# Backward row layouts by DMA transposes, with a chunk's columns in blocked order

## The chip, the cores and the metric

The kernel runs on one core of a Trainium2 chip. The metric is the device time of one execution in microseconds (us); lower is better. A core has five instruction streams that matter here: TensorE (PE in the profile; its weight loads are PEld), VectorE (DVE), ScalarE (ACT), GpSimd (POOL) and SyncE (SP). SyncE does no arithmetic: in this kernel it issues most of the DMA transfers, all DMA transposes among them.

## The reference, cut to what matters

The reference is the forward pass of a small joint network and its gradient for all seven inputs. All tensors are bfloat16.

```python
h  = gelu(conv3(x,  w1))[:, ::2, :]        # B=2, T=16000, D=256, kernel of 3 taps
f  = gelu(conv3(h,  w2))[:, ::2, :]        # 4000 rows of f in each batch
fe = f @ w_f ;  ge = g @ w_g               # g: 8 rows in each batch
j  = tanh(fe[:, :, None, :] + ge[:, None, :, :])
out = j @ w_o                              # [2, 4000, 8, 256]
out, vjp = jax.vjp(forward, x, w1, w2, g, w_f, w_g, w_o)
return out, *vjp(grad_out)                 # grad_out: [2, 4000, 8, 256]
```

A matmul on TensorE contracts over the partition axis. The gradients of the activations contract over channels, so they need a tensor with channels on the partitions ("columns": one column for each time step). The gradients of the weights contract over time, so they need the same tensor with time steps on the partitions ("rows"). The whole argument is about how one is made from the other.

## The kernel before

The 4,000 time steps of each batch are worked off in chunks of up to 512. A small static scheduler (`op(engine, cost, ...)`) gives each operation its engine and its place in that engine's stream when the program is built. These are the parts that the change touches; `P` is 128, `KT` is 2 (256 channels are two halves of 128), `NB` is 4 blocks of 128 steps.

A row layout can be made in two ways. The first is a DMA transpose from SBUF to SBUF. If the buffer has exactly `n*P` columns, one transpose does both halves; a buffer with a padding column (for the neighbour that a 3-tap convolution needs) takes one transpose for each half:

```python
    def dma_rows(name, cls, g_, SRC, off, keys, nb=None, at=None):

        n = (chunks[g_][3] + off_extra.get(name, 0) * (chunks[g_][1] == last_ci[chunks[g_][0]]) + P - 1) // P
        R = buf(cls, [P, KT * NB * P], BF16, name)
        view = lambda: R[:, 0:KT * n * P].rearrange("p (k b q) -> p k b q", k=KT, q=P)
        R.rows = lambda m, bl: view()[:m, :, bl, :]
        R.cols = lambda m, bl, d2: view()[:m, d2, bl, :]
        st[g_][name] = R
        if SRC.shape[-1] == n * P:
            dma("SP", lambda: R[:].rearrange("p (g q) -> p g q", q=P), lambda: SRC[:].rearrange("p k w -> p (k w)"),
                r=[(SRC, k) for k in [0, 1] + keys], w=[R], bytes_=KT * n * P * P * 2, new=[R], transpose=True, nb=nb, at=at)
            return R
        for kt in range(KT):
            dma("SP", lambda kt=kt: view()[:, kt], lambda kt=kt: SRC[:, kt, off:off + n * P],
                r=[(SRC, k) for k in [kt] + keys], w=[(R, kt)], bytes_=n * P * P * 2, new=[R] if kt == 0 else [],
                transpose=True, nb=nb, at=at)
        return R
```

The second is TensorE: 128x128 transposes into PSUM, and a copy back into SBUF by ACT or DVE.

```python
    def to_rows(cls, SRC, off, n, keys):
        dst = buf(cls, [P, NB, D], BF16, cls.upper())
        dst.rows = lambda m, bl: dst[:m, bl, :]
        ps = psum(BF16)
        nbl = (n + P - 1) // P

        def trs(e):
            for bl in range(nbl):
                m = min(P, n - bl * P)
                for kt in range(KT):
                    nc.tensor.transpose(out=ps[:m, (bl * KT + kt) * P:(bl * KT + kt + 1) * P],
                                        in_=SRC[:, kt, off + bl * P:off + bl * P + m], identity=ident[:])
        op("PE", c_pe([P] * (nbl * KT)), trs, r=[(SRC, k) for k in keys] + [ident], w=[ps], new=[ps, dst])
        # [cut: evac() of ps into dst, on ACT or DVE]
```

Before, the row layouts of GHo and GHe (the gradients at the odd and even steps of h) take the second way:

```python
        GHoR = to_rows("rows", GHo, 0, Wsp, [0, 1, "z"])
        tick()
        GHeR = to_rows("rows", GHe, 1, Wsp, [0, 1, "z"])
        tick()
```

grad_out is read twice from DRAM: once as rows (GO_R) and once, transposed by the DMA on the way, as columns (GOT):

```python
    def load_got(g_, u, at):
        b, ci, c0, W = chunks[g_]
        GOT = buf("got", [P, KT, CW], BF16, "GOT")
        dma("SP", lambda: GOT[:, :, :W], lambda: grad_out[b, c0:c0 + W, u, :], r=[], w=[GOT], bytes_=W * D * 2, new=[GOT],
            transpose=True, at=at)
        st[g_].setdefault("GOT", {})[u] = GOT
```

A shifted tap reads the same padded buffer one column further on (`off` is 1 or 0):

```python
        gfk = [(GF, 0), (GF, 1), (GF, "h"), (GF, "z")]
        for mt in range(KT):
            ps = psum()

            def mms(e, mt=mt, ps=ps):
                for k, (i, off, kt) in enumerate([(i, off, kt) for i, off in ((0, 1), (2, 0)) for kt in range(KT)]):
                    mm(ps[:, :Ws], W2T[:, i, kt, mt * P:(mt + 1) * P], GF[:, kt, off:off + Ws], k == 0, k == 3)
            pe_first(mt == 0, "gho", c_pe([Ws] * 4), mms, r=gfk + [(WT, 1), (WT, 2)], w=[ps], new=[ps] + ([GHo] if mt == 0 else []))
            op("DVE", c_dve(Ws), lambda e, mt=mt, ps=ps: nc.vector.scalar_tensor_tensor(
                out=GHo[:, mt, 0:Ws], in0=S["G1o"][:, mt, 1:1 + Ws], scalar=1.0, in1=ps[:, :Ws], op0=ALU.add, op1=ALU.mult),
               r=[(S["G1o"], mt), (S["G1o"], "h"), ps], w=[(GHo, mt)])
            tick()
```

## Time and profile before

| | before |
|---|---|
| median of 4 runs | 820.42 us (820.27 to 822.75) |
| span in the profile | 817.6 us |
| busy: PE, DVE, ACT, POOL | 783.5, 749.1, 737.7, 184.1 us |
| sum of PE's work by columns | 774.6 us |
| DMA transposes and plain copies issued by SP | 351 and 215, issuing for 676 us |

The page's first part gives each engine's busy time, its share of the span and its instructions. The queue lines give packets, MB, and packet time as a share of the 16 DMA engines' time.

```profile
PE 783.5 (96%) x6082; PEld 580.1 (71%) x6172; DVE 749.1 (92%) x1703; ACT 737.7 (90%) x1198; POOL 184.1 (23%) x393
...
q1 hardware_dynamic: 347732, 128.93, 77.0%
```

Three engines stand at 90% or more, so the shares alone don't tell which binds. PE's list of waits does: in us in total, number of waits, longest. These are its first lines.

```profile
PE ps L308 <- DMA W<-in_w_dram: 3.0, 1, 3.0
PE GWO L308 <- ACT JR L628: 3.0, 4, 1.0
PE ps L308 <- DMA GOT<-in_grad_out_dram: 2.7, 1, 2.7
PE ps L308 <- DMA NFR<-NGFE: 1.8, 2, 1.6
PE ps L308 <- DMA GFR<-GF: 1.8, 2, 1.1
```

All lines of this list together are some 20 us of 818. Between 120 and 780 us PE is busy 653.76 of 660 us; the columns are window, length, then busy time and instructions of PE, PEld, DVE, ACT and POOL, PE's clock, DMA share and GB/s.

```profile
0.00:120.00 120.00, 101.72 (x707) 67.27 (x719) 100.68 (x248) 103.42 (x174) 25.65 (x56) 0.97 0.99 213
120.00:780.00 660.00, 653.76 (x5113) 489.72 (x5191) 625.21 (x1380) 619.58 (x995) 146.50 (x310) 1.00 1.01 227
```

A busy PE may still be a slow PE, so I also computed its least work. Starts of back-to-back matmuls stand 109 ns apart at 256 columns, 215 to 216 at 512 and 55 to 56 at 128, which is columns/2.4 + 2.5 ns. The Trainium skill ("TensorE: Matmul & The Clock Gate", section "Wait — 56ns, not 53.3ns?") states the same formula for a warm array, with a floor of about 25 ns; the trace agrees. Summed over the program's matmuls, this is 774.6 us. Time minus this work is time lost, and comparing the two at each weight load shows where: 28.0 us by the point where 120 us of work are done, only 3.2 us between 120 and 740 us of work, 4.0 us from there to the last matmul, and 7.7 us after it.

The groups that the change removes from PE and ACT, by shape (busy us, mean ns of one | idle before):

```profile
L502 PE MATMUL psb<-ident,GHo 128*128 128x128 bf16 x128 | 10.3, 219 | 0.0
L502 PE MATMUL psb<-ident,GHe 128*128 128x128 bf16 x128 | 10.1, 219 | 0.0
L316 ACT COPY ROWS<-psb 128x1024 bf16<-128x1024 bf16 x27 | 27.6, 1024 | 0.0
L316 ACT COPY ROWS<-psb 128x512 bf16<-128x512 bf16 x6 | 3.5, 584 | 0.6 <-PE psb L502 0.6
```

The 219 ns of one transpose is its latency; its cost in the stream is the 55 to 56 ns between starts.

### The profile page before, as it was taken

What the parts mean: (1) busy time and instruction counts of PE and PEld (TensorE: products, weight loads), DVE (VectorE), ACT (ScalarE), POOL (GpSimd) and SP (SyncE); (2) the same over time, 40 slices, a digit from 0 to 9 for tenths busy, and PEclk for the clock granted to TensorE, in tenths of its full rate; (3) what the DMA queues carried; (4) which work ended last, traced back from release to release, by engine and by line L of the source; (5) the groups of instructions that cost most, each with busy time, mean ns of one, the idle gap of its engine ahead of it and who ended that gap; (6) DMA issues with size and microseconds to landing.
All of it is one profiled execution on the core that took longest, in us unless ns stands there. A gap on an engine that the chain in (4) does not pass through costs nothing. (4 is left out here: it accounts for less than half of the span.)

```text
span 817.6 us, 17525 instructions
## 1 busy us (share of the span) xinstructions
PE 783.5 (96%) x6082; PEld 580.1 (71%) x6172; DVE 749.1 (92%) x1703; ACT 737.7 (90%) x1198; POOL 184.1 (23%) x393
## 2 busy tenths in 40 slices
PE   7888989999999999999999999999999999999995
PEld 5555657676776867777777677686777858788883
DVE  3999989998999989997989999998989989998883
ACT  5999989999899998998899999999899999998861
POOL 2111311212121211233131213121121211223241
PEclk9999999999999999999999999999999999999999
DMA  9989999999999898988999999999999897998562
GB/s 187 217 184 208 241 239 218 294 235 245 235 221 260 215 243 187 268 207 211 205 218 228 261 238 230 254 200 259 219 270 233 204 240 215 251 194 207 145 158 82
DMA packets 364444, 180.42 MB, mean 221 GB/s; under 512 B 308964, under 2 KB 344072, under 8 KB 364356
## 3 DMA queue, kind: packets, MB, share of 16 engines
q1 hardware_dynamic: 347732, 128.93, 77.0%
q0 software_dynamic: 15840, 49.98, 20.2%
q8 instruction: 48, 0.79, 0.4%
q10 hardware_dynamic: 784, 0.39, 0.2%
q14 instruction: 40, 0.33, 0.2%
HBM read 54.44 MB, written 50.34 MB: 128 GB/s over the span
## 5 line engine op out<-in xcount | busy, mean ns | idle before, releaser
L608 ACT ACTIVATE JT<-FE,GE 128x512 bf16<-128x512 bf16 (+2 forms) x288 | 187.3, 681 | 0.3
L333 POOL DMA_DIRECT2D out_dram<-OUT_SB x136 | 94.7, 696 | 410.0 <-ACT OUT_SB L316 348.9
L308 PE MATMUL ps<-WO,JT 128*128 128x256 bf16 x1024 | 153.8, 273 | 3.6 <-ACT JT L608 1.5
L670 DVE SCALAR_TENSOR_TENSOR NGZ<-JSQ,ps 128x512 f32<-128x512 bf16 (+2 forms) x252 | 153.8, 613 | 1.3 <-PE ps L308 1.3
L308 PE MATMUL ps<-GOT,WT 128*128 128x512 bf16 (+2 forms) x521 | 141.2, 348 | 3.6 <-DMA GOT<-in_grad_out_dram 2.7
L628 ACT ACTIVATE JR<-JR 128x1024 bf16<-128x1024 bf16 x128 | 136.2, 1070 | 5.8 <-DVE JR L621 5.3
L308 PEld LDWEIGHTS <-JT 128*128 128x128 bf16 x1024 | 99.4, 98 | 54.3 <-ACT JT L608 2.9
L308 PE MATMUL GWO<-GO_R,JR 128*128 128x256 bf16 x1024 | 132.7, 273 | 3.1 <-ACT JR L628 3.0
L316 ACT CAST OUT_SB<-ps 128x512 bf16<-128x512 f32 x214 | 127.4, 598 | 7.1 <-PE ps L308 6.9
L678 DVE TENSOR_TENSOR ZS<-ZS,NGZ 128x512 f32<-128x512 f32 (+2 forms) x216 | 132.8, 618 | 0.3
L660 ACT ACTIVATE JSQ<-JT 128x1024 bf16<-128x1024 bf16 (+2 forms) x117 | 113.0, 965 | 14.4 <-DVE NGZ L670 14.0
L308 PEld LDWEIGHTS <-JR 128*128 128x128 bf16 x1028 | 99.6, 98 | 20.5 <-ACT JR L628 5.1
L308 PEld LDWEIGHTS <-WT 128*128 128x128 bf16 x864 | 82.2, 98 | 42.0 <-DMA GOT<-in_grad_out_dram 3.0
L308 PEld LDWEIGHTS <-W 128*128 128x128 bf16 x648 | 62.5, 99 | 59.8 <-issue 3.5
L308 PE MATMUL ps<-XC,W 128*128 128x512 bf16 (+2 forms) x418 | 92.4, 352 | 1.8 <-DVE NGZ L670 0.8
L308 PE MATMUL ps<-ROWS,X 128*128 128x256 bf16 x768 | 92.6, 273 | 0.6 <-ACT ROWS L316 0.5
L621 DVE TENSOR_TENSOR JR<-FER,GEB 128x1024 bf16<-128x1024 bf16 x128 | 87.9, 690 | 0.5 <-ACT FER L316 0.4
L446 DVE SCALAR_TENSOR_TENSOR g_s<-g_sq,ps 128x512 bf16<-128x512 bf16 (+2 forms) x108 | 66.2, 615 | 18.4 <-ACT HTo L444 13.3
L308 PEld LDWEIGHTS <-X 128*128 128x128 bf16 x768 | 75.0, 98 | 10.2 <-issue 0.6
L726 DVE TENSOR_TENSOR ACC<-ACC,ps 128x512 f32<-128x512 f32 x96 | 64.3, 685 | 11.8 <-PE ps L308 11.7
L308 PE MATMUL ps<-WT,GHo 128*128 128x256 bf16 x384 | 73.3, 273 | 0.5 <-DVE GHo L782 0.2
L308 PE MATMUL ps<-WT,GHe 128*128 128x256 bf16 x384 | 73.3, 273 | 0.4
(132 smaller groups left out, 1179.5 us busy)
## 6 DMA issues: line engine op xcount, KB each, us to landing
GO_R<-in_grad_out_dram SPq DMA_DIRECT2D x120, 256.0 KB, 4.1
out_dram<-OUT_SB POOLq DMA_DIRECT2D x120, 256.0 KB, 4.3
X<-in_x_dram SPq DMA_DIRECT2D x60, 320.0 KB, 4.6
out_dram<-GX_SB POOLq DMA_DIRECT2D x60, 256.0 KB, 3.6
GOT<-in_grad_out_dram SPq DMA_TRANSPOSE x144, 4.3
out_dram<-g_sq SPq DMA_DIRECT2D x9, 128.0 KB, 1.8
GO_R<-in_grad_out_dram SPq DMA_DIRECT2D x8, 128.0 KB, 3.4
out_dram<-OUT_SB POOLq DMA_DIRECT2D x8, 128.0 KB, 3.4
```

What stands on the lines that cost most here:

```text
L308: nc.tensor.matmul(ps_ap, lhsT=lhsT, rhs=rhs, start=start, stop=stop)
L316: nc.scalar.copy(out=dst(), in_=src())
L333: return eng_.dma_start(out=out(), in_=in_())
L446: op("DVE", c_dve(W), lambda e, mt=mt, ps=ps: nc.vector.scalar_tensor_tensor(out=s[:, mt, :W], in0=sq[:, mt, :W], scalar=1.0, in1=ps[:, :W ...
L608: op("ACT", c_act(W, ptr=True), lambda e, j=j, mt=mt: nc.scalar.activation(out=JT[:, j, mt, :W], in_=S["FE"][:, mt, :W], func=ACT.Tanh, bi ...
L621: op("DVE", c_dve(n * 2 * D, 0.5), lambda e, lo=lo, n=n, m=m, JR=JR: nc.vector.tensor_tensor(out=JR[:m, lo % 2:lo % 2 + n], in0=S["FER"][: ...
L628: op("ACT", c_act(n * 2 * D), lambda e, lo=lo, n=n, m=m, JR=JR: nc.scalar.activation(out=JR[:m, lo % 2:lo % 2 + n], in_=JR[:m, lo % 2:lo % ...
L660: nc.scalar.activation(out=JSQ[:, :, :W], in_=JT[:, j, :, :W], func=ACT.Square)
L670: op("DVE", c_dve(W) + 6, lambda e, d2=d2, ps=ps, u=u, zap=zap, JSQ=JSQ: nc.vector.scalar_tensor_tensor(out=zap(), in0=JSQ[:, d2, :W], sca ...
L678: op("DVE", c_dve(W), lambda e, d2=d2, dst=dst, NGZ=NGZ: nc.vector.tensor_tensor(out=dst[:, d2, :W], in0=ZS[:, d2, :W], in1=NGZ[:, :W], op ...
L726: op("DVE", c_dve(512), lambda e: nc.vector.tensor_tensor(out=acc_ap().rearrange("p k d -> p (k d)"), in0=acc_ap().rearrange("p k d -> p ( ...
```

## The change

The intent is to take the last backward row layouts off TensorE and ScalarE and to give them to the DMA.

If row 4p+a of a chunk of 512 stands in column 128a+p ("blocked order"), the row before it stands in column 128(a-1)+p when a is 1, 2 or 3: a whole block to the left. Only block 0 needs a true shift by one column, and a copy of one block makes it (`shift`, on GpSimd or VectorE). So no buffer needs a padding column, every buffer is `n*P` columns long, and one DMA transpose makes any row layout. Blocked order also lets one DMA load four consecutive rows into a partition. And the columns of grad_out (GOT) come by DMA transpose from the rows already in SBUF, not from DRAM again.

The core of the diff, with cuts marked. The helper for buffers without padding, and the shifted block:

```diff
+    def colbuf(cls, g_, name):
+
+        n = KT * nb_of[g_] * P
+        b_ = buf(cls, [P, KT * CW], BF16, name)
+        b_.view = lambda t_: t_[:, 0:n].rearrange("p (k w) -> p k w", k=KT)
+        return b_
[cut]
+    def shift(cls, g_, name, src, reads, halo, halo_reads, at=None):
+
+        S_ = buf(cls, [P, KT, P], BF16, name)
+        s0 = (nb_of[g_] - 1) * P if whole[g_] else 0
+
+        def cp(e):
+            (nc.gpsimd if e == "POOL" else nc.vector).tensor_copy(out=S_[:, :, 1:P], in_=src(s0, s0 + P - 1))
+        op(("POOL", "DVE"), (430.0, c_dve(KT * (P - 1), 0.25)), cp, r=reads, w=[(S_, "m")], new=[S_], at=at)
+        if halo is None:
+            op("POOL", 120.0, lambda e: nc.gpsimd.memset(S_[:, :, 0:1], 0.0), w=[(S_, "h")], at=at)
+        else:
+            op("POOL", 200.0, lambda e: nc.gpsimd.tensor_copy(out=S_[:, :, 0:1], in_=halo()), r=halo_reads, w=[(S_, "h")], at=at)
+        return S_
+
+    def back(g_, S_, T_, n):
+
+        r0 = 0 if whole[g_] else P - 1
+        return [(0, lambda kt: S_[:, kt, :]), (P, lambda kt: T_[:, kt, r0:r0 + n - P])]
```

GOT from GO_R:

```diff
-    def load_got(g_, u, at):
-        b, ci, c0, W = chunks[g_]
-        GOT = buf("got", [P, KT, CW], BF16, "GOT")
-        dma("SP", lambda: GOT[:, :, :W], lambda: grad_out[b, c0:c0 + W, u, :], r=[], w=[GOT], bytes_=W * D * 2, new=[GOT],
-            transpose=True, at=at)
-        st[g_].setdefault("GOT", {})[u] = GOT
[cut]
+    def load_got(g_, up, h, at):
+        S = st[g_]
+        if h == 0:
+            S.setdefault("GOT", {})[up] = buf("got", [P, NB, 2, KT, P], BF16, "GOT")
+        GOT, GO = S["GOT"][up], S["GO"][up, h]
+        dma("SP", lambda: GOT[:, 2 * h:2 * h + 2].rearrange("p a u k q -> p (a u k) q"),
+            lambda: GO[:].rearrange("p a u v -> p (a u v)"), r=[GO], w=[(GOT, h)], bytes_=2 * P * 1024,
+            new=[GOT] if h == 0 else [], transpose=True, at=at)
```

One transpose for each row layout:

```diff
-    def dma_rows(name, cls, g_, SRC, off, keys, nb=None, at=None):
-
-        n = (chunks[g_][3] + off_extra.get(name, 0) * (chunks[g_][1] == last_ci[chunks[g_][0]]) + P - 1) // P
-        R = buf(cls, [P, KT * NB * P], BF16, name)
-        view = lambda: R[:, 0:KT * n * P].rearrange("p (k b q) -> p k b q", k=KT, q=P)
-        R.rows = lambda m, bl: view()[:m, :, bl, :]
-        R.cols = lambda m, bl, d2: view()[:m, d2, bl, :]
-        st[g_][name] = R
-        if SRC.shape[-1] == n * P:
-            dma("SP", lambda: R[:].rearrange("p (g q) -> p g q", q=P), lambda: SRC[:].rearrange("p k w -> p (k w)"),
-                r=[(SRC, k) for k in [0, 1] + keys], w=[R], bytes_=KT * n * P * P * 2, new=[R], transpose=True, nb=nb, at=at)
-            return R
-        for kt in range(KT):
-            dma("SP", lambda kt=kt: view()[:, kt], lambda kt=kt: SRC[:, kt, off:off + n * P],
-                r=[(SRC, k) for k in [kt] + keys], w=[(R, kt)], bytes_=n * P * P * 2, new=[R] if kt == 0 else [],
-                transpose=True, nb=nb, at=at)
+    def dma_rows(name, cls, g_, src, reads, n, nb=None, at=None):
+
+        R = buf(cls, [P, KT * n * P if cls == "hrs" else KT * NB * P], BF16, name)
+        R.view = lambda t_: t_[:, 0:KT * n * P].rearrange("p (k b q) -> p k b q", k=KT, q=P)
+        R.rows = lambda m, bl: R[:m, :, bl, :]
+        R.cols = lambda m, bl, d2: R[:m, d2, bl, :]
+        dma("SP", lambda: R.t[:, 0:KT * n * P].rearrange("p (g q) -> p g q", q=P), src, r=reads, w=[R],
+            bytes_=KT * n * P * P * 2, new=[R], transpose=True, nb=nb, at=at)
```

A shifted tap becomes two matmuls, 128 columns from the shifted block and the rest from the buffer itself, and GHo's operation on DVE splits likewise:

```diff
-                for k, (i, off, kt) in enumerate([(i, off, kt) for i, off in ((0, 1), (2, 0)) for kt in range(KT)]):
-                    mm(ps[:, :Ws], W2T[:, i, kt, mt * P:(mt + 1) * P], GF[:, kt, off:off + Ws], k == 0, k == 3)
-            pe_first(mt == 0, "gho", c_pe([Ws] * 4), mms, r=gfk + [(WT, 1), (WT, 2)], w=[ps], new=[ps] + ([GHo] if mt == 0 else []))
-            op("DVE", c_dve(Ws), lambda e, mt=mt, ps=ps: nc.vector.scalar_tensor_tensor(
-                out=GHo[:, mt, 0:Ws], in0=S["G1o"][:, mt, 1:1 + Ws], scalar=1.0, in1=ps[:, :Ws], op0=ALU.add, op1=ALU.mult),
-               r=[(S["G1o"], mt), (S["G1o"], "h"), ps], w=[(GHo, mt)])
+                for kt in range(KT):
+                    mm(ps[:, :Ws], W2T[:, 0, kt, mt * P:(mt + 1) * P], GF[:, kt, 0:Ws], kt == 0, False)
+                pts = back(g_, GFS, GF, Ws)
+                for k, (lo, f) in enumerate(pts):
+                    for kt in range(KT):
+                        mm(ps[:, lo:P if k == 0 else Ws], W2T[:, 2, kt, mt * P:(mt + 1) * P], f(kt), False,
+                           k == len(pts) - 1 and kt == KT - 1)
+            pe_first(mt == 0, "gho", c_pe([Ws] * 2 + [P, Ws - P] * 2), mms, r=gfk + [(WT, 1), (WT, 2)], w=[ps], new=[ps] + ([GHo] if mt == 0 else []))
+            r0 = 0 if wh else P - 1
+            for q_, (lo, hi, in0) in enumerate(((0, P, lambda mt=mt: S["G1S"][:, mt, :]),
+                                                (P, Ws, lambda mt=mt: S["G1o"][:, mt, r0:r0 + Ws - P]))):
+                op("DVE", c_dve(hi - lo), lambda e, mt=mt, ps=ps, lo=lo, hi=hi, in0=in0: nc.vector.scalar_tensor_tensor(
+                    out=GHo[:, mt, lo:hi], in0=in0(), scalar=1.0, in1=ps[:, lo:hi], op0=ALU.add, op1=ALU.mult),
+                   r=[S["G1S"] if q_ == 0 else (S["G1o"], mt), ps], w=[(GHo, (mt, q_))])
```

And the two layouts that leave TensorE:

```diff
-        GHoR = to_rows("rows", GHo, 0, Wsp, [0, 1, "z"])
+        hold_ = S["go"] if g_ < 2 else ()
+        if wh:
+            X5 = [load_x9(b, c0, nb_of[g_], h, t0 + dt * 0.2, hold_) for h in range(nb_of[g_] // 2)]
+            xrow = lambda m, bl, f, d2: X5[bl // 2][:m, bl % 2 * 4 + f, d2 * P:(d2 + 1) * P]
+        else:
+            X5 = [load_x5(b, c0 + bl * P, min(P, Ws - bl * P), t0 + dt * 0.2, hold_) for bl, m in sblk]
+            xrow = lambda m, bl, f, d2: X5[bl][:m, f, d2 * P:(d2 + 1) * P]
+        pad_tail(g_, GHo, Ws)
+        ghok = [(GHo, (mt, q_)) for mt in range(KT) for q_ in range(2)] + [(GHo, "z")]
+        ghek = [(GHe, 0), (GHe, 1), (GHe, "z"), GHS]
+        GHoR = dma_rows("GHoR", "rows", g_, lambda: GHo[:].rearrange("p k w -> p (k w)"), ghok, nb_of[g_])
         tick()
-        GHeR = to_rows("rows", GHe, 1, Wsp, [0, 1, "z"])
+        GHeR = col_rows("GHeR", "rows", g_, GHe, ["z"])
```

Cut: the same treatment of x, h and f in the forward pass, wider loads of x for the gradient of w1, stores with a row stride, buffer counts (GO_R from 6 to 7, row layouts from 3 to 4, GOT from 8 small to 3 large ones), and GO_R's loads 0.3 chunk earlier. The last chunk of each batch, of 160 rows, keeps the plain order, with the same shifted block in front.

## The prediction

> **What bounds the kernel now.** TensorE. The page shows PE busy 96%, DVE 92%, ACT 90% and DMA near 90% or more in most slices; three readings decide. (1) Matmul starts in the trace stand 109 ns apart for 256 columns, 215 to 216 for 512, 55 to 56 for 128: columns/2.4 + 2.5 ns. Summed over the built program's 6,168 matmuls this is 774 us of the 818 us span. (2) The list of waits for PE holds only about 20 us, mostly before 120 us. (3) By stretches, PE is 98.6 to 99.3% busy from 120 to 780 us. Other losses: the start (about 28 us over the ideal in the first 120 us) and a tail of about 20 us (last row transposes and stores). DMA is loaded but does not limit: packet times sum to over 100% in many 2 us windows because packets overlap, throughput averages 221 GB/s and peaks near 390. The Trainium skill ("SBUF — State Buffer", shared port pair) warns that GpSimd and some VectorE modes block each other; here a bf16 tensor_scalar of 1024 columns took 427 ns alone, 455 beside a GpSimd copy or memset, so I count little for the new GpSimd copies.
>
> **What the change does, costed.**
> - PE: 256 transposes of GHo and GHe go (55 ns each, 14 us). Splitting the shifted taps adds about 280 matmuls but no columns (2.5 ns each, under 1 us). Sum after: 761.5 us, **-12.8 us** on the binding engine.
> - ACT: 33 ROWS copies go (27 x 1.02 + 6 x 0.58 = 31 us); the static schedule gives ACT 8 more OUT_SB evictions, 3 more JSQ and a few others: net about -25 us, 738 to 713.
> - DVE: GHo's operation splits in two (durations fit 151 ns + 1.05 ns per column: +0.15 us x 36 = 5.4 us), 28 shift copies land here (estimate 0.2 us, 5.6 us), about 9 us go to ACT: net about +2 us, 749 to 751. That is near 98% mid-run: almost a second bound.
> - POOL: 62 shift copies, estimate 0.4 us, +27 us on an engine 23% busy.
> - DMA: GOT comes from SBUF in the same number of 256 B packets (HRe, read from SBUF, lands in 4.3 us like GOT from DRAM). HRs shrinks (-3 MB), GHoR and GHeR come (+8.2 MB): about 20,000 more packets of 18 ns, some 23 us over 16 engines. X loads shrink by 2 MB. SP's queue has 456 rows instead of 481.
> - GOT now waits for its GO_R load (4.1 us to landing), but loads issue 0.3 chunk (about 15 us) earlier and PE's new order uses the first GOT later; this should hide.
>
> **On the critical path:** the PE saving nearly whole, since PE is saturated; the ACT saving hardly; perhaps 1 to 3 us given back where DVE is full. Start and tail about even: the tail gets GHoR and GHeR transposes but loses the second halves of NFR and GFR.
>
> **Predicted:** 820.45 - 12.8 = 807.7 us, range 801 to 815. Chances: faster by over 2% 0.20, within 2% 0.77, slower 0.03.
>
> **What would show it.** PE work down 1.6%, PE still 98 to 99% busy mid-run; no ROWS copies; ACT near 713 us, DVE near 751; GOT landing near 4.3 us; PE waits for DMA about 10 us.
>
> **What would make it wrong.** DVE as the new bound (PE gaps ended by DVE): 812 or more. SBUF-sourced transposes slower, or SP's queue held up behind GOT's wait for GO_R: PE waits for GOT, GHoR or GHeR. Blocked moving reads slower than 215 ns per 512 columns. Faster if ACT's relief shortens the first 120 us.

## The result, and the profile after

The changed kernel takes 807.13 us (median of 4 runs, 806.70 to 808.01) against 820.42 us, and its results are correct. Executions over 1.5% slower than the fastest of the same kernel are left out of the means. Ratios in this document are the mean time of one kernel's runs over that of the other's of the same rounds, so not quite the ratio of the medians quoted. Here it is 0.9833, with a 95% interval of 0.9813 to 0.9853: 1.7% less time, within 2%. The prediction was 807.7 us.

The page's first part and the queue of the transposes, after:

```profile
PE 773.3 (96%) x6156; PEld 578.0 (72%) x6196; DVE 750.4 (93%) x1754; ACT 713.0 (89%) x1175; POOL 211.4 (26%) x456
...
q1 hardware_dynamic: 366644, 133.25, 85.4%
```

PE's busy time fell by 10.2 us and ACT's by 24.7; DVE's stayed, POOL's rose by 27.3. The first waits of PE:

```profile
PE GWO L342 <- ACT JR L715: 6.8, 4, 3.1
PE psb L581 <- ACT FE L353: 3.2, 8, 0.6
PE ps L342 <- DMA W<-in_w_dram: 3.0, 1, 3.0
PE ps L342 <- DVE NGFE L770: 1.4, 1, 1.4
PE psb L581 <- DVE FE L358: 1.4, 2, 1.2
```

No line for GOT, NFR, GFR, GHoR or GHeR is left: in this profile, what the DMA transposes, it transposes in time. The short waits for FE have grown, from 1.7 us in 5 waits before to 4.6 us in 10. The same stretches as before:

```profile
0.00:120.00 120.00, 104.79 (x779) 73.06 (x784) 106.72 (x266) 107.53 (x182) 29.39 (x69) 0.97 1.05 220
120.00:780.00 660.00, 653.68 (x5238) 492.93 (x5271) 630.01 (x1447) 601.66 (x987) 177.27 (x375) 1.00 1.08 237
```

PE is as busy mid-run as before, over matmuls that do more of what is wanted. Of the groups shown of before, none is left. What answers to them is the split operation of GHo, the shifted blocks and the new transposes (DMA lines: number, us from issue to landing).

```profile
L883 DVE SCALAR_TENSOR_TENSOR GHo<-G1o,ps 128x384 bf16<-128x384 bf16 x28 | 15.2, 543 | 0.0
L883 DVE SCALAR_TENSOR_TENSOR GHo<-G1S,ps 128x128 bf16<-128x128 bf16 x36 | 10.0, 278 | 0.5 <-PE ps L342 0.5
...
L293 POOL COPY GFS<-GF 128x254 bf16<-128x254 bf16 x13 | 7.0, 538 | 9.0 <-DVE GF L852 9.0
```

```profile
GOT<-GO_R SPq DMA_TRANSPOSE x128, 5.0
...
GHoR<-GHo SPq DMA_TRANSPOSE x18, 4.0
GHeR<-GHe SPq DMA_TRANSPOSE x18, 4.6
```

The span in terms of PE's work, for the profiled run of each kernel that the argument uses (one profile each; between alike kernels the first 120 us vary by a few us). Each row sums to the span, up to rounding:

| us | PE's work by columns | lost up to 120 us of work | 120 to 740 us of work | 740 us to last matmul | after it | span |
|---|---|---|---|---|---|---|
| before | 774.6 | 28.0 | 3.2 | 4.0 | 7.7 | 817.6 |
| after | 761.8 | 23.2 | 7.4 | 4.0 | 9.2 | 805.6 |
| e1_pe_rows | 776.1 | 22.1 | 7.2 | 4.4 | 10.8 | 820.6 |
| e3_pe_alone | 776.1 | 22.3 | 9.7 | 4.0 | 8.9 | 821.0 |
| e4_act_alone | 761.8 | 27.6 | 10.7 | 3.9 | 9.2 | 813.1 |
| e7_two_issues | 761.8 | 32.1 | 39.6 | 10.8 | 6.5 | 850.9 |
| e6c_fer_one_issue | 755.1 | 25.5 | 11.0 | 4.0 | 9.9 | 805.6 |
| e8_no_jsq | 755.1 | 20.9 | 15.9 | 6.5 | 10.3 | 808.8 |

So the 12.0 us between the two spans are: -12.8 of PE's work, -4.8 at the start, +4.2 mid-run, +1.4 after the last matmul. The prediction's sum came out, with two errors of opposite sign beside it. That they cancel, so that the number is met within 0.6 us, is luck; the 12.8 us are not.

### The profile page after: what moved, and what is told of

Read it like the earlier page. It is cut to its first block, busy times and chain, and to the rows that moved or that the text cites. A ratio compares the mean times of both kernels' runs of the same rounds, so it can differ in the third digit from the quotient of the medians.

```text
span 805.6 us, 17603 instructions
## 1 busy us (share of the span) xinstructions
PE 773.3 (96%) x6156; PEld 578.0 (72%) x6196; DVE 750.4 (93%) x1754; ACT 713.0 (89%) x1175; POOL 211.4 (26%) x456
## 3 DMA queue, kind: packets, MB, share of 16 engines
q1 hardware_dynamic: 366644, 133.25, 85.4%
## 4 chain that ended last, share of the span: by engine, by line
PE 69%; DVE 11%; ACT 10%; issue 5%; DMA 2%; POOL 1%; SPq 1%; POOLq 0%; ACTq 0%; DVEq 0%
PE ps L342 58%; PE GWO L342 10%; DVE NGZ L762 2%; DVE g_s L528 2%; ACT g_s L534 2%; ACT JT L695 2%; ACT OUT_SB L353 1%; ACT g_sq L524 1%; ACT JR L715 1%; DVE ZS L770 1%; ACT FE L353 1%; PE psb L581 1%; DMA XC<-in_x_dram 1%; POOL out_dram L370 1%; ACT JSQ L752 1%
## 5 line engine op out<-in xcount | busy, mean ns | idle before, releaser
L342 PE MATMUL ps<-GOT,WT 128*128 128x512 bf16 (+3 forms) x640 | 151.8, 334 | 1.4 <-ACT GX_SB L355 0.2
L762 DVE SCALAR_TENSOR_TENSOR NGZ<-JSQ,ps 128x512 f32<-128x512 bf16 (+2 forms) x252 | 151.4, 606 | 1.4 <-PE ps L342 0.9
L353 ACT CAST OUT_SB<-ps 128x512 bf16<-128x512 f32 x222 | 134.2, 611 | 15.7 <-PE ps L342 15.6
L715 ACT ACTIVATE JR<-JR 128x1024 bf16<-128x1024 bf16 x128 | 138.7, 1088 | 5.4 <-DVE JR L708 5.1
L752 ACT ACTIVATE JSQ<-JT 128x1024 bf16<-128x1024 bf16 (+2 forms) x122 | 118.2, 969 | 15.3 <-DVE NGZ L762 14.0
L342 PEld LDWEIGHTS <-WT 128*128 128x128 bf16 x1000 | 88.2, 98 | 37.9 <-issue 3.1
L342 PEld LDWEIGHTS <-W 128*128 128x128 bf16 x792 | 69.6, 98 | 55.1 <-DMA W<-in_w_dram 3.2
L342 PE MATMUL ps<-XC,W 128*128 128x512 bf16 (+4 forms) x432 | 92.2, 342 | 0.7
L528 DVE SCALAR_TENSOR_TENSOR g_s<-g_sq,ps 128x512 bf16<-128x512 bf16 (+2 forms) x108 | 66.0, 612 | 12.6 <-ACT HTo L526 10.1
L534 ACT ACTIVATE g_s<-g_s 128x1024 bf16<-128x1024 bf16 (+2 forms) x54 | 52.6, 976 | 15.5 <-DVE g_s L528 15.5
L342 PE MATMUL ps<-WT,GHe 128*128 128x256 bf16 x348 | 66.2, 273 | 0.0
```

The source lines that it names most:

```text
L342: nc.tensor.matmul(ps_ap, lhsT=lhsT, rhs=rhs, start=start, stop=stop)
L353: nc.scalar.copy(out=dst(), in_=src())
L528: op("DVE", c_dve(W), lambda e, mt=mt, ps=ps: nc.vector.scalar_tensor_tensor(out=s[:, mt, :W], in0=sq[:, mt, :W], scalar=1.0, in1=ps[:, :W ...
L534: op("ACT", c_act(N), lambda e: nc.scalar.activation(out=s[:, :, :W], in_=s[:, :, :W], func=ACT.Tanh, scale=c), r=[s], w=[s], at=late)
L715: op("ACT", c_act(n * 2 * D), lambda e, lo=lo, n=n, m=m, JR=JR: nc.scalar.activation(out=JR[:m, lo % 2:lo % 2 + n], in_=JR[:m, lo % 2:lo % ...
L752: nc.scalar.activation(out=JSQ[:, :, :W], in_=JT[:, j, :, :W], func=ACT.Square)
```

## The experiments

Twelve kernels ran. My theory was the prediction's: TensorE's columns set the time. Its rivals were that the saving came from ACT's copies, from the rest of the change, or that the DMA had become the limit. All results passed the comparison with the reference. Before was run again beside each: 819.6 to 820.2 us on the first chips, 822.7 on the last. The static scheduler plans anew for each kernel, so with an edit the order on the engines changes a little too, and a few operations move between ACT and DVE (in e3, eight go from ACT to DVE).

### e1_pe_rows: undo only the two layouts

The changed kernel, with GHo's and GHe's rows made by TensorE and copied by ACT or DVE again.

```diff
-GHoR = dma_rows("GHoR", "rows", g_, lambda: GHo[:]..., ghok, nb_of[g_])
+GHoR = to_rows("rows", GHo, 0, nb_of[g_] * P, [...])
-GHeR = col_rows("GHeR", "rows", g_, GHe, ["z"])
+GHeR = to_rows("rows", GHe, 0, nb_of[g_] * P, [...])
```

> The changed kernel with one part undone: the row layouts of GHo and GHe come from PE transposes and ACT/DVE copies again, everything else (blocked columns, GOT from SBUF, 9-row X loads) stays. Column sum on PE 776.25 us against 761.96. Theory (the gain is PE column work): 807.1 + 14.3 = about 821 us. Rival A (the gain is the ROWS copies that ACT lost): about 820 as well. Rival B (the gain is in the other parts: fewer X bytes, GOT from SBUF, fewer DMA issues): 807 to 809 us.

Measured: 822.34 us (820.98 to 824.09), ratio to before 1.0016 (0.9973 to 1.0059). The whole gain is gone. The rest of the change, blocked order and GOT from SBUF and all its new copies, brings nothing by itself and costs nothing. The table shows that it isn't idle inside: e1 loses 5.9 us less than before at the start and 4.0 us more mid-run, as the changed kernel does. These two belong to the rest of the change, and they nearly cancel.

### e3_pe_alone: add only TensorE's work back

The changed kernel with 256 transposes of GHo and GHe on TensorE whose result nobody reads.

```diff
+def idle_trs(SRC, keys):     # into a PSUM buffer, no copy
+    for bl in range(nb_of[g_]):
+        for kt in range(KT): nc.tensor.transpose(out=ps[...], in_=SRC[:, kt, bl*P:(bl+1)*P], identity=ident[:])
```

> The changed kernel plus the 256 PE transposes of GHo and GHe into PSUM that nobody reads; no copy on ACT or DVE, row layouts still by DMA. Column sum 776.25 us. Theory: 807.1 + 14.3 = 820 to 822 us. Rival A (ACT's copies): 807 to 810 us. Rival B: 807 to 810 us.

Measured: 820.29 us (820.08 to 822.76), ratio to before 0.9996 (0.9960 to 1.0033), against 0.9833 for the changed kernel. The transposes' starts alone, 256 x 55.8 ns = 14.3 us, cost 13 us. TensorE's columns are the limit, nearly one to one.

### e4_act_alone: add only ScalarE's work back

The changed kernel with 72 idle copies on ACT, some 40 us of them: more than the 31 us of copies that the change took away.

```diff
+def idle_copy(SRC, keys):    # for kt in range(KT):
+    op("ACT", c_act(n, True), lambda e: nc.scalar.copy(out=ps[:, 0:n], in_=SRC[:, kt, 0:n]), ...)
```

> The changed kernel plus copies of GHo and GHe on ACT (72 of 512 or 256 columns into PSUM that nobody reads, about 40 us of ACT time, rather more than the 31 us of the ROWS copies); no PE transposes. Column sum on PE unchanged, 761.96 us. Theory: 807 to 810 us (the scheduler hands evictions to DVE, a little more stalling). Rival A: 815 to 820 us.

Measured: 813.50 us (811.20 to 815.01), ratio 0.9904 (0.9865 to 0.9944): 6.4 us more than the changed kernel. This is between what the two theories expected. ACT was busy 742.3 us in this run, about as in before. So ScalarE isn't quite off the critical path. In the one profile of each that the table shows, e4 loses 4.4 us more at the start and 3.3 us more mid-run; before 50 us PE ran at half clock for 13.7 us in it, against 6.8 us in the changed kernel, so this isn't the price of ACT's mid-run work alone. But its effect doesn't add to TensorE's: e1, which has both, is only 2 us slower than e3, which has TensorE's alone, and 15 us slower than the changed kernel.

### e5_fer_later: the waits for FE

The table shows 4.2 us given back mid-run, and the list of waits shows PE waiting for FE before its transposes. Here those transposes are scheduled 0.1 chunk later.

```diff
+F.now = t0 + (A_AT[2] + 0.1) * dt
 S["FER"] = to_rows("fer", FE, 0, nb_of[g_] * P, [0, 1, "z"])
```

> The changed kernel with one priority changed: the PE transposes of FE, for which PE waits 0.6 to 0.8 us once per chunk in the middle of the run, are placed 0.1 of a chunk (about 5 us) later. Column sum unchanged, 761.96 us. If those waits are what the change gave back in the middle (about 4 us more lag than in the kernel before from 120 us on): 803 to 805 us and the steps of 0.6 us gone. If they only stand where PE would have waited for ACT or DVE anyway: 806 to 808 us.

Measured: 808.04 us (806.78 to 808.88), ratio 0.9854 (0.9828 to 0.9880): no gain. Other short waits took the place of these. The place of the FE transposes isn't the cause; why mid-run loses 4 us more than before stays open, apart from e1's finding that it comes with the rest of the change.

### e2_dma_rows_only: the two layouts alone, in the kernel before

If the rest of the change brings nothing, is it needed? Here the kernel before gets its GHo and GHe rows by its own `dma_rows`. Its padded buffers take two transposes for a layout, one for each half. One transpose for both was refused, because the source with its padding isn't a plain two-dimensional block.

```diff
-GHoR = to_rows("rows", GHo, 0, Wsp, [0, 1, "z"])
+GHoR = dma_rows("GHoR", "rows", g_, GHo, 0, ["z"])
-GHeR = to_rows("rows", GHe, 1, Wsp, [0, 1, "z"])
+GHeR = dma_rows("GHeR", "rows", g_, GHe, 1, ["h", "z"])
```

> The kernel before with one part of the change alone: the row layouts of GHo and GHe by DMA transposes (two each, because the columns stay padded), nothing else changed, still 3 row buffers. Column sum on PE 760.45 us against 774.75. Theory: 820.4 - 14.3 = about 806 us, up to 809 if three row buffers are too few for the longer DMA latency. Rival A: about 806 too. Rival B: 818 to 820 us.

Measured: 840.37 us (834.14 to 850.94); the fast runs against before's 1.0209 (1.0125 to 1.0292). It takes 14 us of columns from TensorE (760.5 us are left), the change 12.8 us, and it is 2% slower than before. All that I had expected of it was wrong. Its profile fell in its slowest run (850.94 us), so I rest nothing on its sums. What it pointed to was waits of PE for DMA transposes, and that is what the next runs test. SP issued 423 transposes and 215 copies here, against 351 and 215 before and 309 and 185 in the changed kernel.

### e2b_more_rows: is it the buffers?

As e2, with four buffers for row layouts in place of three, as the changed kernel has, and six of GOT in place of eight so that SBUF holds them.

> As e2_dma_rows_only (the kernel before with GHoR and GHeR by DMA), but with four row buffers in place of three, paid for with six GOT buffers in place of eight. Theory S (e2 lost its gain because SP's queue is full: it issued for 782 us of its 849): the number of issues is the same, so still 825 to 840 us. Theory R (the third and fourth layouts wait for a free row buffer): 806 to 812 us.

Measured: 839.50 us (837.43 to 848.63), ratio 1.0261 (1.0199 to 1.0322). No better: row buffers aren't the cause. PE's list of waits begins:

```profile
PE ps L308 <- DMA GHeR<-GHe: 9.2, 5, 3.8
```

For GOT, whose buffers were cut, PE waited 1.6 us in all.

### e2c_loads_pool: take the plain loads off SP

As e2, with `LOADQ` (the queue of the plain loads) moved from SP to GpSimd. This leaves SP the transposes and a few stores. Moving transposes to a second queue was no choice without waits between the two: the Trainium skill ("DMA: Bandwidth & Descriptors", section "Silent corruption: two transposing streams in flight at once") warns that two streams of transposes in flight together can corrupt each other. No run here shows it.

> As e2_dma_rows_only, with its three row buffers and eight GOT buffers, but the plain loads of GO_R and X are issued by GpSimd, which leaves SP 423 transposes and 9 stores (about 670 us of issuing). Theory S (SP's queue is full in e2): 806 to 815 us. Theory R (row buffers): still 825 to 840 us.

Measured: 903.30 us (892.66 to 917.73), ratio 1.0974 (1.0894 to 1.1054), missed by both theories. The run is confounded: the loads come from another queue now, and the transposes got slower. GOT landed after 6.1 us in the median, against 4.4 in e2, and SP issued for 853 us, against 782, although it had 206 copies fewer to issue (both profiles fell in their kernel's slowest run, so I take only the direction from them). Why is not shown. So the length of an issue isn't fixed, and the run doesn't tell what I wanted to know.

### e7_two_issues: twice the transposes, the same bytes

This is the run that decides. The changed kernel, with each row layout cut into two DMA transposes of half the size. The packets that carry data, the bytes, the buffers and the arithmetic stay, and the number of transposes on SP's queue goes from 309 to 435. Two things change beside it: 4,032 packets of 4 bytes come with the new issues, 1% of all packets, and the scheduler puts part of PE's matmuls in another order.

```diff
-dma("SP", R (n blocks of both halves), src, transpose=True)
+for h in range(2):
+    dma("SP", half h of R, half h of src, transpose=True)
```

> The changed kernel with every row layout (HRo, HRe, FR, NFR, GFR, GHoR, GHeR) issued as two DMA transposes of half the size in place of one: the same packets and bytes, 435 transposes on SP in place of 309 (e2 has 423), column sum unchanged, 761.96 us. Theory S (what made e2 slow is the number of issues on SP's queue): 822 to 840 us, PE waiting for GHeR, GHoR and NFR. Theory D (it is the packets on the DMA engines, of which e2 has hardly more than this kernel): 807 to 811 us.

Measured: 852.33 us (850.46 to 861.54), ratio 1.0424 (1.0354 to 1.0495): 45 us more than the changed kernel (852.33 - 807.13), and more than before. The list of PE's waits, over the whole span, begins:

```profile
PE ps L342 <- DMA NFR<-NGFE: 9.7, 6, 3.3
PE ps L342 <- DMA GOT<-GO_R: 9.7, 7, 2.4
PE ps L342 <- DMA GHeR<-GHe: 7.4, 7, 2.5
```

And yet each transpose, once issued, mostly lands sooner than in the changed kernel:

```profile
NFR<-NGFE SPq DMA_TRANSPOSE x36, 5.5
...
GHoR<-GHo SPq DMA_TRANSPOSE x36, 3.6
GHeR<-GHe SPq DMA_TRANSPOSE x36, 4.0
```

(In the changed kernel NFR landed after 6.5 us, GHoR after 4.0, GHeR after 4.6.) So it isn't the transfer that comes late; it is its turn. The traces show the turn itself. Between 120 and 780 us, the median time from the end of the last operation that writes GHo to the issue of its transpose was 4.7 us in the changed kernel and 12.4 us here (GHeR 5.3 and 14.5 us, NFR 2.4 and 9.5 us). Here 82 of these 83 issues began within 0.2 us of the end of the issue before, so it was SP that was busy. (In e2b the three are 10.6, 12.2 and 10.1 us.) The trace's records of SP's issuing instructions say why; in ns, shortest, median and longest, first in the changed kernel, then here:

```profile
L368 SPq DMA_TRANSPOSE GHoR<-GHo x18: 1189/1407/2394, 76.1 to 789.9; - x18
L368 SPq DMA_TRANSPOSE GHoR<-GHo x36: 1167/1219/2024, 84.1 to 835.9; - x36
```

By size, the shortest transpose of 256 KB from SBUF took 1.23 us to issue and the shortest of 128 KB 1.19 us, in both kernels. The mean over the layouts that were cut fell only from 1.82 to 1.42 us. Together SP's issues took 784 of 851 us here, 688 of 806 us in the changed kernel: 126 more issues of the same bytes took 96 us more. SP issues in order, so a transpose that PE needs waits behind all that was put before it. The clock adds to the loss: between 120 and 780 us three of PE's gaps here were followed by 3.41 us at half clock each, and none in the changed kernel.

### e6_fer_dma: the next layout too

TensorE still transposes FE into rows (FER), 128 transposes, 7 us. The changed kernel, with FER by two DMA transposes for each chunk:

```diff
-S["FER"] = to_rows("fer", FE, ...)
+for kt in range(KT):
+    dma("SP", FER[:, blocks, half kt], FE[:, kt, ...], transpose=True)
```

> The changed kernel with the last PE transposes gone too: FER comes from FE by two DMA transposes per chunk, so 36 more issues on SP (about 46 us, 734 of some 800 us) and 128 fewer PE transposes, column sum 754.8 us, and 14 fewer ACT/DVE copies. Theory (PE column work, and the FE waits go with it): 807.1 - 7.1 - 4 = about 796 to 800 us. If SP's queue is the next limit, as theory S has it for e2: 803 us or more, with PE waits for DMA.

Measured: 817.05 us (813.28 to 825.40), ratio 0.9981 (0.9907 to 1.0055): 10 us slower than the changed kernel, with 7 us less work for TensorE.

### e6c_fer_one_issue and e6d_fer_from_third: the same with one issue

In e6c FE is stored block by block, so that one transpose does a whole chunk: 325 transposes, not 345. In e6d the first two chunks keep TensorE's transposes (323).

> As e6_fer_dma (FER by DMA, no PE transposes of FE), but FE lies in blocks so that each whole chunk's FER is one DMA transpose: 325 transposes on SP in place of 345, with the same packets. Column sum 755.3 us. Theory S: the mid-run waits of e6 shrink, 800 to 806 us, the start still late because JR waits for FER (e6 lost 9 us between 20 and 40 us, the changed kernel 5.5). Theory D: 812 to 817 us as e6.

> As e6c_fer_one_issue, but the first two chunks keep the PE transposes of FE, so that the start is the changed kernel's. Column sum 755.9 us. If e6's loss at the start comes from FER's DMA latency, about 3 us under e6c: 797 to 803 us by theory S, 809 to 813 by theory D. If it comes from something else, as e6c.

Measured: e6c 805.92 us (801.35 to 808.84), ratio 0.9829 (0.9789 to 0.9869); e6d 806.77 us (804.52 to 811.45), ratio 0.9852 (0.9814 to 0.9890). Twenty issues fewer, and the other layout of FE that allows them, brought back the 10 us of e6, but neither beats the changed kernel (0.9833). The 7 us that TensorE was spared are lost again elsewhere: the table shows e6c losing 2.3 us more at the start, 3.6 us more mid-run and 0.7 us more after the last matmul.

### e8_no_jsq: what holds e6c back?

e6c without the squares of tanh (JSQ): this takes work from ACT and DVE only. The gradients are wrong; that the run passed the comparison all the same says only how small these values are against the tolerance.

```diff
-op(("ACT", "DVE"), ..., jsq, ...)              # JSQ = JT * JT
-out=zap(), in0=JSQ[:, d2, :W], ...             # (JSQ - 1) * ps
+out=zap(), in0=JT[:, j, d2, :W], ...
```

> e6c_fer_one_issue with the JSQ operations taken out (the operation that read JSQ reads JT instead, so gradients are wrong on purpose). PE's work by columns (755.3 us) and the transposes and copies on SP's queue (325 and 185) stay; about 118 us of ACT's work and 14 us of DVE's go. Theory C (with PE's work cut to 755 us, DVE and ACT are now what keeps the time at 806): 785 to 798 us. Theory S (SP's queue of transposes keeps it there): 801 us or more, with PE still waiting for FER or other row layouts by DMA. Between 798 and 801 us would be both.

Measured: 808.15 us (804.24 to 812.65), ratio 0.9824 (0.9767 to 0.9881); before took 822.71 us on this chip.

```profile
PE 773.5 (96%) x6076; PEld 571.5 (71%) x6076; DVE 729.8 (90%) x1715; ACT 625.1 (77%) x1062; POOL 211.5 (26%) x448
```

ACT was spared 88 us and DVE 16 us against e6c, and the time didn't move. So neither of them holds it. PE's waits between 120 and 780 us begin:

```profile
PE ps L342 <- DMA GOT<-GO_R: 5.3, 5, 2.0
PE GWO L342 <- ACT JR L726: 1.9, 4, 0.8
```

In the changed kernel no mid-run wait was for a DMA. SP issued for 730 of 809 us here. With TensorE's work at 755 us the path of the transposes is what is left. The traces lean to SP's issuing: between 120 and 780 us GHeR's transpose was issued 8.8 us after its source was ready in e6c and 12.1 us in e8 (medians), against 5.3 us in the changed kernel. But whether it is the issuing or the DMA behind it, this run can't settle: e6c and e8 also move some 16,000 packets more than the changed kernel, and a long issue may itself be one that waits for room.

## Why the prediction was right

| step of the prediction | predicted | measured |
|---|---|---|
| PE's work by columns, saved | 12.8 us | 12.8 us (774.6 to 761.8); e3: putting it back costs 13 us |
| ACT busy after | 713 us | 713.0 us |
| DVE busy after | 751 us | 750.4 us |
| DVE mid-run | near 98% | 630.0 of 660 us, 95% |
| POOL | +27 us | +27.3 us |
| DMA packets | +20,000, +23 us of packet time over 16 engines | +18,914; the queue's share rose from 77.0% of 817.6 to 85.4% of 805.6 us, +58 us |
| GOT from issue to landing | near 4.3 us | 5.0 us |
| PE's waits for DMA | about 10 us | 4.2 us (W 3.0, JR's load 1.2) |
| given back mid-run | 1 to 3 us | 4.2 us |
| start and tail | about even | -4.8 and +1.4 us |
| ACT's relief on the critical path | hardly | 40 us of ACT work cost 6.4 us (e4) |
| time | 807.7 us | 807.13 us |

**The main term was right for its reason.** TensorE bounds the kernel; the change takes 12.8 us of columns from it, and the time falls by about that. e3 shows it with hardly anything else changed, and e1 shows that the rest of the change sums to nothing.

**Four terms were off, none by enough to matter.** The start gained 4.8 us that I had called even, and mid-run gave back 4.2 us where I had 1 to 3. My reason for the 1 to 3 us, a full DVE, isn't what the waits show: mid-run, waits ended by DVE come to 0.8 us, and those ended by ACT's copies of FE to 3.2 us (and e5 gained nothing by moving these). e1 shows both in a kernel that has the rest of the change but not its saving. At the start one event is gone: PE's wait for GOT at 111 us. In the kernel before, the timeline of PE shows it (start, duration, work, then idle time before it):

```profile
113.95 0.61 PE L308 MATMUL ps<-GOT,WT 128*128 128x512 bf16 x2 [2.71 <-DMA GOT<-in_grad_out_dram]
```

And the stretches around it show that it cost twice; the last three columns are clock, DMA share and GB/s.

```profile
110.00:115.00 5.00, 2.29 (x17) 1.63 (x19) 5.00 (x12) 4.62 (x7) 1.28 (x2) 1.00 1.04 226
115.00:118.40 3.40, 3.40 (x12) 1.52 (x11) 0.46 (x2) 0.58 (x2) 0.00 (x0) 0.51 0.89 291
```

From 115.08 us on, for 3.41 us, PE ran at half clock. The Trainium skill ("TensorE: Matmul & The Clock Gate", section "Why this matters for your kernels") says to keep PE's idle gaps below about 3 us for this reason; here a wait of 2.7 us was already followed by it. But this doesn't explain the 4.8 us. The kernel before has one more such stretch, from 12.7 us on, and the changed kernel two, from 29.0 and 42.6 us on: 6.8 us at half clock in each. And PE's waits for JR grew from 3.0 to 6.8 us, more than the 2.7 us of the wait for GOT. What the start gained by stays open; no run isolates it. ACT's relief was mis-sized as "hardly": e4 puts a price on it, about 0.16 us for each us of ACT's copies (6.4/40; 0.22 by the 29.3 us that ACT's busy time rose by, since the scheduler moved other work off it), though not one that adds to TensorE's. And the new transposes' packets took more time than I gave them: I priced a 256-byte packet at its median of 18 ns, but the mean was 23.5 ns before and 25.1 ns after.

**What the prediction did not see** is why the change is built as it is. It counted SP's issues ("456 rows instead of 481", where the trace counts 494 transposes and copies instead of 566) and gave them no price. Yet this is what makes the saving reachable: the same saving without blocked order, with two issues for a layout (e2), makes the kernel before 2% slower, and the changed kernel with two issues for a layout (e7) is 5.6% slower than with one (852.33/807.13). The rest of the change gains no time; it cuts the number of issues and so leaves SP room for the new ones. HRo and GFR go from 36 to 18 transposes, HRs from 36 to 22, HRe, FR and NFR from 22 to 18 each, GOT from 144 to 128, and the loads of x from 70 to 40. The Trainium skill ("Perfetto Trace Analysis", section "What "DMA-bound" means") names the sequencer that issues DMAs as one of the things a kernel can be bound by. I read the DMA engines' load and overlooked this second one, and my "what would make it wrong" had it only as a queue held up behind one wait.

## What to carry to other kernels

Price each transfer twice: for the DMA engines by its packets, and for the queue that issues it by its count, and sum the second over the whole run. The count alone doesn't give that sum: a transpose took 1.85 us to issue in the mean in the changed kernel and 1.55 us in e7. Before moving work to a queue, look for a layout in which one issue does what two did; the layout may gain nothing by itself and still decide whether the move pays. When three engines are over 90% busy, add idle work to one of them at a time: the price of a microsecond on each, here about 0.9 us on TensorE (13/14.3) and some 0.2 us on ScalarE, tells which binds.

## What the Trainium skill lacked or had wrong

- "DMA: Bandwidth & Descriptors", section "Issuing engines are not separate DMA queues", calls the time to initiate a DMA "usually small relative to the DMA itself". For DMA transposes it wasn't: at least 1.19 us and 1.45 us in the median to issue, against 3.6 to 6.5 us to landing (medians of the groups of 18 and more), and 688 us of 806 for all of SP's issues. No page gives a measured time for issuing a transpose on this chip (cycle counts of unnamed "previous generations" are all there is), or says that the least time hardly falls with size: 1.23 us for 256 KB and 1.19 us for 128 KB. 126 more issues of the same bytes took 96 us more of SP's time and 45 us more of the kernel's.
- "Perfetto Trace Analysis", section "What "DMA-bound" means", advises large descriptors for a bound sequencer. e7 kept the packets that carry data as they were, raised the number of transposes from 309 to 435, and took 45 us more; the number of DMA instructions is the other lever, and the page doesn't name it there.
- "TensorE: Matmul & The Clock Gate", section "Why this matters for your kernels", puts the gap that costs the clock at about 3 us. Here a wait of 2.7 us was followed by 3.41 us at half clock, and in the changed kernel a gap of 2.06 us (at 25.7 us) was too, while one of 2.98 us (at 10.0 us) was not: no single length decides.
- "SBUF — State Buffer", section "Who interferes with whom", whose shared port pair the prediction drew on, held. In the changed kernel, alone and beside a GpSimd copy, VectorE's NGZ of 512 columns (one input in SBUF) took 675 and 676 ns, ZS of 512 columns (two inputs in SBUF) 679 and 774 ns, and the tensor_scalar of 1024 columns on g_sq 429 and 517 ns. With 33 operations on ZS, g_sq and g_s beside a copy, this is some 3 us of VectorE's time, as little as the prediction counted on.
